# Which engine gives out the first small load: ScalarE in place of Sync

## The chip, the core and the metric

The kernel runs on one core of one Trainium2 chip. A core has TensorE (PE in the profile, with its weight loads as PEld), VectorE (DVE), ScalarE (ACT), GpSimd (POOL) and SyncE (SP). Each has its own queue of instructions, worked off in order, and they wait for each other through semaphores. Transfers between the chip's memory (HBM) and the on-chip buffers are given out by an engine's queue as DMA issues and carried out by 16 DMA engines. The metric is device time in microseconds for one execution. Before the change the median of three runs is 377.19 us (376.98 to 377.27).

## The reference

One decoding step: two sequences (B = 2), one token each, width D = 512. The token is normalised and goes through attention over a window of 2048 cached positions in 32 heads of 128, and through a bilinear feed-forward block of width F = 1376; both are added to the input. All numbers are 32-bit floats.

```python
W = min(4096, max(256, Sk // 4))                       # Sk = 8192, so W = 2048
xn = _layernorm(x, axis=-1)
q = (xn @ wq).reshape(B, 1, 32, 128).transpose(0, 2, 1, 3)
k = k_cache[:, :, Sk - W:, :]
v = v_cache[:, :, Sk - W:, :]
scores = jnp.einsum("bhqd,bhkd->bhqk", q, k) * (128 ** -0.5)
p = _softmax(scores, axis=-1)
o = jnp.einsum("bhqk,bhkd->bhqd", p, v)
attn = o.transpose(0, 2, 1, 3).reshape(B, 1, 4096) @ wo
h = jnp.einsum("bsd,df->bsf", xn, w_gate) * jnp.einsum("bsd,df->bsf", xn, w_up)
out = x + attn + jnp.einsum("bsf,fd->bsd", h, w_down)
```

Every cached key and value and every weight is used once, so some 160 MB go from HBM to the chip and little is computed on each byte.

## The kernel before

All inputs but the last rows of w_down are laid out as one long stream in HBM, in the order in which the kernel wants them. `blocks()` (line 86) lists the pieces: one small load, with the key `("f", 0)`, and then big loads of up to 128 x 15872 numbers (some 8 MB), with keys `("s", i)`. The small load goes to a tile of its own, `first`, 128 x 542 numbers: x, two small tables of ones (`pick`, `rows`) and the columns of wq for head 0. The big ones go to tiles called `step`, of which there are three buffers (`BUFS = 3`).

`pump()` (line 175) gives out loads as long as a buffer is free. It is called once at the start, where it gives out `first` and three big loads, and then from `done()` (line 198) each time that all fields of a big load have been used. All of these are issued by Sync, line 196. Behind the first call, line 213, Sync also issues four small loads of the last rows of w_down into `wd_tail`. Sync's queue is in order, so a load waits in it for its buffer, and the loads behind wait as well.

The first big load holds the rest of wq for heads 1 to 3 and the keys of heads 0, 1 and 2. The second holds the gate and up weights and the keys of head 3, the third values and more.

The work around the start runs like this. VectorE sums x from `first`, TensorE spreads the sums over the partitions with a matrix of 1/512 (`mean_w`), VectorE subtracts and squares, TensorE sums again, ScalarE takes the square root, VectorE scales, and copies the normalised token out to a wide tile `xnb`. Then `project_first(0)` (line 272) multiplies `xnb` with the wq of head 0 into `tr` on TensorE. From there, for each head, `products` (line 304) multiplies the keys with the query on VectorE, in place, `sums` (line 312) reduces them to scores on VectorE and then marks the keys as used; softmax follows on GpSimd and ScalarE, and the weighted sum of the values and the output projection on TensorE. When `sums(2)` is done the first buffer is free and Sync can issue the fourth big load into it.

Most instructions pass through a helper (`InOrder`, line 113) which keeps each engine's program in the order of the code, so the profile gives line 128 for nearly all of them; they are told apart by their tiles. The order of heads and of the big loads is worked out ahead by `groups()` and `packed()`; neither has to do with the small load.

Of the kernel before, what the change touches and what calls it, by code (L numbers as in the profile page):

```python
# [143 lines left out]
def kernel(  # L144
# [7 lines left out]
    pe, dve, act, sp = (InOrder(tc, e) for e in (nc.tensor, nc.vector, nc.scalar, nc.sync))  # L152
# [17 lines left out]
    tiles, used, left, got = {}, {}, {}, {}  # L170
# [4 lines left out]
    def pump():  # L175
        nonlocal held
        while todo:
            key, fields, at = todo[0]
            if key not in tiles:
                if key[0] == "f":  # L180
                    n = sum(w for _, _, w in fields)
                    tiles[key] = const.tile([P, n], F32, name="first")
                elif held == BUFS:
                    return
                else:
                    held += 1
                    tiles[key] = steps.tile([P, STEP], F32, name="step")
                used[key] = 0
            todo.pop(0)
            c0 = used[key]  # L190
            for kind, i, w in fields:
                got[kind, i] = (tiles[key][:, used[key] : used[key] + w], key)
                used[key] += w
            c1 = used[key]
            src = stream[at : at + P * (c1 - c0)].rearrange("(p i) -> p i", p=P)
            sp.dma_start(tiles[key][:, c0:c1], src)

    def done(kind, i):
        nonlocal held
        _, key = got.pop((kind, i))  # L200
        left[key] -= 1
        if left[key] == 0 and key[0] != "f":
            del tiles[key]
            held -= 1
            pump()

    pump()
    xT = got["x", 0][0].rearrange("p (b c) -> p b c", b=B)
    pick = got["pick", 0][0].rearrange("p (r s b) -> p r s b", s=2, b=B)
# [472 lines left out]
```

## Time and profile before

| | |
|---|---|
| median of three runs | 377.19 us (376.98 to 377.27) |
| profiled execution: span from first to last instruction | 375.6 us |
| the same execution's time beyond its span | not given; the median lies 1.6 us above the span |
| VectorE busy | 294.5 us, 78% |
| TensorE busy | 256.8 us, 68% |
| ScalarE busy | 57.1 us, 15% |
| moved by DMA | 159.70 MB, mean 425 GB/s over the span |
| Sync's DMA queue q1 | 159.54 MB, 98.5% of the 16 engines' span |
| small load `first` | 271.0 KB, issue to landing 2.8 us |

In the profile "DMA step<-in_stream_dram" is a big load and "DMA first<-in_stream_dram" the small one. SPq is Sync's queue giving out a DMA; the time beside it is that of the issue, and not of the transfer. In the DMA table q1 is the queue of the loads that Sync gives out, q8 and q14 are fetches of instructions; a row has packets, megabytes, and the time of the packets as a share of 16 engines over the stretch asked for. A packet counts with its whole time in the slice in which it begins, so over short stretches a share can be above 100%. The slices divide the stretch asked for into 40 equal parts.

### The profile page before, as it was taken

The numbers are of one execution on the slowest core, as the hardware profiler recorded it, in microseconds if no ns is written. First come the engines' busy times: TensorE is split into PE (matmuls) and PEld (weight loads), VectorE is DVE, ScalarE is ACT, GpSimd is POOL, SyncE is SP. The second block draws the span as 40 slices with busy tenths as digits, with TensorE's granted clock in tenths as the row PEclk, the third lists the DMA queues.
The fourth block names the chain that finished last, engine by engine and source line by source line (L and its number), as shares of the span: only waits on it lengthen the run. The fifth ranks groups of instructions, "written<-read, shape, count | busy, mean of one in ns | idle before, by whom it ended". The sixth has DMA issues, their size and how long they took to land.

```text
span 375.6 us, 2894 instructions
## 1 busy us (share of the span) xinstructions
PE 256.8 (68%) x1106; PEld 89.1 (24%) x1106; DVE 294.5 (78%) x144; ACT 57.1 (15%) x259; POOL 25.2 (7%) x74
## 2 busy tenths in 40 slices
PE   3166696884587881685858905896556864699896
PEld 3132123231222220121222202222211221133243
DVE  3069999369979569999369999894699999999750
ACT  1002011110201210021112002112010210112131
POOL 1000000000001000000100000010000000000010
PEclk9999697799576897598968875889666898689999
DMA  8999999999999999999999999999999999999995
GB/s 344 419 444 466 452 414 440 433 433 434 421 427 433 433 433 440 435 426 433 433 433 429 433 433 440 433 435 433 433 440 433 441 433 433 433 433 413 419 415 229
DMA packets 4092, 159.70 MB, mean 425 GB/s; under 512 B 462, under 2 KB 718, under 8 KB 1136
## 3 DMA queue, kind: packets, MB, share of 16 engines
q1 hardware_dynamic: 4080, 159.54, 98.5%
q8 instruction: 8, 0.13, 0.1%
q14 instruction: 4, 0.03, 0.0%
HBM read 159.47 MB, written 0.07 MB: 425 GB/s over the span
## 4 chain that ended last, share of the span: by engine, by line
DMA 65%; PE 18%; DVE 14%; ACT 1%; issue 1%; SPq 0%; DVEq 0%
DMA step<-in_stream_dram 65%; DVE s L128 7%; DVE step L128 7%; PE o_ps L128 6%; PE q L128 6%; PE acc L128 4%; PE tr L128 2%; ACT o_sb L128 1%; ACT oT L128 0%; DVE m L128 0%; SPq L128 0%; DVE o_out L128 0%; DVE rec L128 0%; DVEq L128 0%
## 5 line engine op out<-in xcount | busy, mean ns | idle before, releaser
L128 DVE TENSOR_TENSOR step<-step,q 128x4096 f32<-128x4096 f32 x31 | 136.8, 4412 | 45.1 <-DMA step<-in_stream_dram 41.1
L128 DVE TENSOR_REDUCE s<-step 128x32 f32<-128x4096 f32 x32 | 141.4, 4419 | 1.1
L128 PE MATMUL o_ps<-step,p 128*16 128x512 f32 x512 | 77.3, 667 | 47.6 <-DMA step<-in_stream_dram 47.5
L128 PE MATMUL q<-step,xnb 128*128 128x512 f32 (+1 forms) x128 | 74.2, 727 | 32.2 <-DMA step<-in_stream_dram 32.2
L128 PEld LDWEIGHTS q<-step,xnb 128*128 128x128 f32 x128 | 28.5, 238 | 81.4 <-issue 65.7
L128 PE MATMUL acc<-step,oT 128*2 128x512 f32 (+1 forms) x88 | 37.9, 590 | 8.6 <-ACT oT L128 8.6
L128 PE MATMUL tr<-first,o_sb 128*128 128x2 f32 (+4 forms) x190 | 29.5, 274 | 15.7 <-ACT o_sb L128 11.9
L128 PEld LDWEIGHTS o_ps<-step,p 128*16 128x16 f32 x512 | 13.6, 100 | 100.8 <-DMA step<-in_stream_dram 57.4
L128 PEld LDWEIGHTS tr<-first,o_sb 128*128 128x128 f32 (+2 forms) x190 | 26.9, 216 | 40.6 <-ACT o_sb L128 34.8
L128 ACT COPY o_sb<-o_ps 128x512 f32<-128x512 f32 x23 | 13.5, 585 | 147.4 <-PE o_ps L128 147.4
L322 POOL PARTITION_ALL_REDUCE mm<-m x32 | 11.4, 357 | 242.1 <-DVE rec L128 136.5
L128 ACT ACTIVATE nm<-mm 128x2 f32<-128x2 f32 x32 | 6.6, 206 | 127.4 <-POOL mm L322 127.4
L128 ACT ACTIVATE p<-s,nm 128x16 f32<-128x16 f32 x64 | 19.1, 300 | 1.0
L338 POOL PARTITION_ALL_REDUCE sum<-rs x32 | 12.7, 398 | 96.3 <-ACT p L128 96.3
L128 PE MATMUL o_ps<-step,xn 128*2 128x512 f32 (+1 forms) x48 | 14.8, 676 | 6.0 <-DMA step<-in_stream_dram 6.0
L128 DVE TENSOR_TENSOR step<-step,tr 128x4096 f32<-128x4096 f32 x1 | 4.4, 4422 | 15.4 <-DMA step<-in_stream_dram 15.4
L128 ACT ACTIVATE oT<-tr,rec 128x1 f32<-128x1 f32 x64 | 12.1, 260 | 27.7 <-PE tr L128 27.7
L128 ACT ACTIVATION_READ_ACCUMULATOR p<-s,nm 128x1 f32 x64 | 11.9, 187 | 0.0
L128 PE MATMUL q<-xnb,mean_w 128*128 128x512 f32 (+4 forms) x26 | 10.5, 512 | 0.0
L128 PEld LDWEIGHTS acc<-step,oT 128*2 128x2 f32 x88 | 4.4, 88 | 21.4 <-ACT oT L128 12.1
L128 DVE RECIPROCAL rec<-sum 128x2 f32<-128x2 f32 x32 | 5.0, 155 | 3.8 <-POOL sum L338 3.8
L128 PE MATMUL acc<-step,hT 128*2 128x128 f32 (+2 forms) x72 | 7.2, 308 | 0.0
(41 smaller groups left out, 43.6 us busy)
## 6 DMA issues: line engine op xcount, KB each, us to landing
step<-in_stream_dram SPq DMA_DIRECT2D x15, 7936.0 KB, 32.2
step<-in_stream_dram SPq DMA_DIRECT2D x1, 7808.0 KB, 39.1
step<-in_stream_dram SPq DMA_DIRECT2D x1, 7680.0 KB, 21.1
step<-in_stream_dram SPq DMA_DIRECT2D x1, 7552.0 KB, 57.8
step<-in_stream_dram SPq DMA_DIRECT2D x1, 4864.0 KB
step<-in_stream_dram SPq DMA_DIRECT2D x1, 3328.0 KB, 19.4
step<-in_stream_dram SPq DMA_DIRECT2D x1, 2304.0 KB, 24.5
step<-in_stream_dram SPq DMA_DIRECT2D x2, 1024.0 KB, 18.0
```

The source lines that it names most:

```text
L128: made = call(*args, **kwargs)
L322: nc.gpsimd.partition_all_reduce(mm, m, P, bass_isa.ReduceOp.max)
L338: nc.gpsimd.partition_all_reduce(sum_t[h], rs, P, bass_isa.ReduceOp.add)
```

## The change

The small load is issued by ScalarE; all other loads stay with Sync.

```diff
@@ -193,7 +193,7 @@
                 used[key] += w
             c1 = used[key]
             src = stream[at : at + P * (c1 - c0)].rearrange("(p i) -> p i", p=P)
-            sp.dma_start(tiles[key][:, c0:c1], src)
+            (act if key[0] == "f" else sp).dma_start(tiles[key][:, c0:c1], src)
```

`key[0] == "f"` is true for the small load alone. The layout of the stream, the tiles and all waits are as before. On Sync, at the head of its program, stood before (the first row is the jump into the kernel's body, `128x542` the small load, the wider ones big loads):

```order
L677 UNCONDITIONAL_BRANCH
L128 DMA first<-in_stream_dram 128x542
L128 DMA step<-in_stream_dram 128x15360
L128 DMA step<-in_stream_dram 128x15616
L128 DMA step<-in_stream_dram 128x15104
L128 DMA wd_tail<-in_tail_dram 25x512
L128 DMA wd_tail<-in_tail_dram 7x512
```

And in the same place now:

```order
L677 UNCONDITIONAL_BRANCH
L128 DMA step<-in_stream_dram 128x15360
L128 DMA step<-in_stream_dram 128x15616
L128 DMA step<-in_stream_dram 128x15104
L128 DMA wd_tail<-in_tail_dram 25x512
L128 DMA wd_tail<-in_tail_dram 7x512
```

The small load is gone and the rest of Sync's program follows one place earlier. On ScalarE, also at the head, stand now (the loads of tables of functions are its own; `st<-tr,eps_t` is the square root of the normalisation, `nm` and `p` belong to the softmax of head 0):

```order
L677 UNCONDITIONAL_BRANCH
L128 DMA first<-in_stream_dram 128x542
L128 ACT_TABLE_LOAD
L128 ACTIVATE st<-tr,eps_t 128x2
L128 ACTIVATE nm<-mm 128x2
L128 ACT_TABLE_LOAD
```

The second row is new: ScalarE gives out the small load ahead of its first table load. The rest of ScalarE's program, and the programs of TensorE, VectorE and GpSimd, are the same.

## The prediction

> **What bounds the kernel now.** I read the page's slices first, then the DMA table of the long middle, the chain of waits at the start, and last the DMA table of very short stretches, where single rows of a transfer can be seen. The first fence has the page's DMA slices and the queue rows for 70 to 350 us.
>
> ```profile
> DMA  8999999999999999999999999999999999999995
> ...
> q1 hardware_dynamic: 2195, 120.92, 99.7%
> q8 instruction: 6, 0.10, 0.1%
> q14 instruction: 4, 0.03, 0.0%
> ```
>
> The 16 DMA engines are full from the second slice to the last but one, and between 70 and 350 us Sync's queue (q1) alone fills 99.7% of them. So the end of the program is the end of one stream of bytes: whatever takes time from the stream moves the end by as much, and work that does not hold up the stream costs nothing. The change touches only the first few microseconds of that stream. Here is the timeline up to 11 us, shortened, and two rows of the page's DMA issues.
>
> ```profile
> 0.72 1.28 ACT L128 ACT_TABLE_LOAD   x1 [0.72 <-PEq L663]
> 0.72 0.38 SPq L128 DMA_DIRECT2D first<-in_stream_dram  x1
> 1.15 1.37 SPq L128 DMA_DIRECT2D step<-in_stream_dram  x3
> 3.54 0.16 DVE L128 TENSOR_REDUCE st<-first 128x2 f32<-128x8 f32 x1 [0.88 <-DMA first<-in_stream_dram]
> 5.62 0.26 ACT L128 ACTIVATE st<-tr,eps_t 128x2 f32<-128x2 f32 x1 [3.62 <-PE tr L128]
> 7.11 3.75 PE L128 MATMUL tr<-first,xnb 128*128 128x128 f32 x16 [1.53 <-issue]
> ...
> step<-in_stream_dram SPq DMA_DIRECT2D x1, 7680.0 KB, 21.1
> ...
> first<-in_stream_dram SPq DMA_DIRECT2D x1, 271.0 KB, 2.8
> ```
>
> The small load lands at 0.72 + 2.8 = 3.5 us. The normalisation and the query of head 0 follow and are done at 7.11 + 3.75 = 10.86 us, that is 7.35 us after the landing. The first big load lands only at 1.15 + 21.1 = 22.3 us. So before the change 11.4 us of slack lie between the query of head 0 and the keys that it meets. The chain of waits shows what VectorE does from there (its rows up to the first buffer's return), with Sync's timeline row of the load that takes the buffer and VectorE's waits between 70 and 79 us.
>
> ```profile
> 22.38 4.43 DVE step L128
> 26.84 4.43 DVE s L128
> ...
> 44.90 4.43 DVE s L128
> ...
> 49.39 0.36 SPq L128 DMA_DIRECT2D step<-in_stream_dram  x1
> ...
> DVE step L128 <- DMA step<-in_stream_dram: 7.8, 1, 7.8
> ```
>
> Three heads one behind the other, 22.38 to 49.33 us (44.90 + 4.43), 26.95 us, then Sync gives out the fourth big load into the freed buffer at 49.39 us. Later VectorE waits 7.8 us for that load, so a delay of VectorE up to that size is swallowed, provided the stream does not run dry meanwhile.
>
> **The start of the stream.** The DMA table for 0 to 4 us, in 40 slices of 0.1 us:
>
> ```profile
> GB/s 0 0 0 0 0 0 0 0 0 0 0 0 0 0 0 0 0 152 130 65 130 217 152 152 369 412 434 918 5067 701 1865 1229 0 614 0 0 0 0 0 0
> DMA packets 160, 1.26 MB, mean 315 GB/s; under 512 B 16, under 2 KB 16, under 8 KB 144
> ```
>
> A packet counts in the slice in which it begins. The 144 - 16 = 128 packets of 2168 bytes are the rows of the small load, eight for each DMA engine; the 16 under 512 bytes are the landing marks; the other 16 are the first rows (61440 bytes) of the first big load. The small rows begin in the slice from 1.7 us, 1.0 us after the issue at 0.72. The big rows begin between 2.7 and 3.4 us, although they were issued at 1.15 and could have begun at about 2.15: they wait behind the small rows, not for Sync. So Sync's 0.43 us (1.15 - 0.72) is not itself on the path. What can be won is that the small rows take 1.0 to 1.6 us, while 0.277 MB would take 0.64 us at the 433 GB/s of the middle (120.92 MB in 280 us is 432): 0.4 to 0.9 us if big rows fill the gaps, say 0.6.
>
> **What the change does, part by part.** (1) One issue leaves Sync's queue; three big and four tail issues move up by 0.43 us. Nobody waits for Sync's own time there, as shown. (2) ScalarE's queue gains one issue of 0.38 us ahead of its table load of 1.28 us, which then ends at 2.4 us instead of 2.0. Its first user starts at 5.62 us; 3.2 us of cover are left, and more if the small load is late. Price: zero. (3) Both queues now issue at 0.72 us, so the rows of both should reach the DMA engines at 1.7 us, and from there each engine has eight rows of 2 KB in one ring and rows of 60 KB in another.
>
> No row shows two such rings side by side. The nearest is the fetch of instructions, which breaks into the same stream from a queue of its own. The fence has the DMA queue rows of windows 0.10 us wide, where the share times 1.6 is the time of the packets that begin in it: first an undisturbed row (from 93.60), then a fetch (from 93.41, with the begin of another engine's row), then the stream's rows that follow fetches (from 93.72, 105.61 and 205.83; from 253.46 two rows, one disturbed and one not).
>
> ```profile
> q1 hardware_dynamic: 1, 0.06, 146.4%
> ...
> q14 instruction: 1, 0.01, 19.3%
> ...
> q1 hardware_dynamic: 1, 0.06, 167.6%
> ...
> q1 hardware_dynamic: 1, 0.06, 185.1%
> ...
> q1 hardware_dynamic: 1, 0.06, 159.9%
> ...
> q1 hardware_dynamic: 2, 0.13, 314.6%
> ```
>
> An undisturbed row takes 2.34 us. The fetch of 8 KB takes 0.31 us, its bytes' worth. The row behind a fetch takes 2.68, 2.96, 2.56 and 5.03 - 2.34 = 2.69 us: 0.34, 0.62, 0.22 and 0.35 us too long, 0.38 in the mean. So the engine does change queues between two rows, and the stream pays at its return.
>
> From this two things follow. First, the small load no longer lands early. If each engine takes one row from each ring in turn, the eighth small row and its landing mark come just about when the eighth big row has gone, so the small load lands with the first big load, at about 22 us instead of 3.5. The Trainium skill says so outright: "DMA: Bandwidth & Descriptors", section "Queues, rings and completion order", has each DMA engine go round robin over the queues that have work, a packet at a time. By that rule the small load lands near 22 us; the fetch rows above agree, though they show single packets only.
>
> Then VectorE begins its first head at 22.3 + 7.35 = 29.7 instead of 22.4 us, 7.3 us later, and the fourth big load is issued 7.3 us later, near 56.7, its rows ready 1.0 us after (as at the start), near 57.7 us. Does the stream have work until then? The DMA slices from 57.30 to 58.42 us, 0.028 us each, show where the engines go over to the fourth load (2268 and more is one of its 63488-byte rows):
>
> ```profile
> GB/s 0 73 0 0 4608 0 0 4682 0 2268 146 0 2341 146 146 0 146 2414 0 146 146 73 2414 146 73 4535 2414 73 0 2414 73 0 2341 73 0 2268 73 0 0 2268
> ```
>
> They go over between 57.4 and 58.4 us. So the first engines would wait 0.3 us, the last none: 0.1 in the mean, with the first rows' latency 0.2. That is the price of a VectorE delay of 7.3 us; each further microsecond of it would cost nearly a whole one. The 7.8 us that VectorE waited for the fourth load then cover the delay, so nothing is late behind it.
>
> Second, the returns. One or two small rows may slip through before the first big row, so I take seven returns per engine at 0.38 us, 2.7 us; all engines pay it and the engine's own rate leaves nothing to catch up with. The ends: nothing (two filled rings may overlap where a lone fetch cannot), and 8 x 0.62 = 5.0 us. I take the 8 KB fetches since they are nearest in size to 2 KB; the 16 KB fetches of q8 are farther.
>
> **The sum.** Start -0.6, returns +2.7, dry stream +0.2: +2.3 us. The profiled span of 375.6 us becomes 377.9. The median of the runs, 377.19, lies 1.6 us above that span; with the same 1.6 us the time is 379.5 us.
>
> **The rivals.** (a) The small load is late, but the change of rings is free. Then -0.6 + 0.2 = -0.4, between -0.9 and +0.2: 376.8 us, the other side. It decides if a return costs less than (0.6 - 0.2) / 7 = 0.06 us. For it: at the start both rings stand full, while a fetch comes alone. Against it: four of four rows behind a fetch were slower by 0.22 us or more. (b) The small load is not held up, because ScalarE's rows reach the engines a microsecond ahead or the engine empties a short ring first. VectorE keeps its times, and 0 to 0.6 us are won: 376.9 us. Against it: ScalarE's first instruction and Sync's first issue both stand at 0.72 us, so no head start is to be seen. A page would have this outcome too: the Trainium skill, "DMA: Bandwidth & Descriptors", section "Issuing engines are not separate DMA queues", says that issuing from several engines saves only the sequencer's time for the issue; here that would be at most 0.43 us, about 376.8 us. (c) The small load is held still longer, a big row of 2.3 us or more beyond the first big load, because its landing mark waits for one more turn. Each such row makes VectorE late beyond its cover: 379.5 + 2.2 = 381.7 us, or 379 with free returns.
>
> **Chances.** The forecast (late, with paid returns) 0.50; (a) 0.25; (b) 0.17; (c) 0.08. A difference of 0.2%, 0.75 us, is about what a measurement can tell from none. The forecast and (c) are slower; of (a) about a quarter is faster and a little slower, of (b) two fifths faster: faster 0.13, same 0.27, slower 0.60. The forecast's own range is 378.1 to 382.0: 377.2 - 0.6 with seven returns of 0.22 (1.5) and no dry stream, to 377.2 - 0.4 with eight of 0.62 (5.0) and 0.2. The range reaches below to (a) and (b) near their best, 376.5, and above past the forecast's end and (c) to 382.5.
>
> **What would show it.** Right: the small load's time to landing near 21 us instead of 2.8; the normalisation and the query of head 0 at 22 to 30 us; VectorE's first head near 30; the first big load landing 1 to 3 us later than 22.3; a short dip of the DMA near 58; VectorE's 7.8 us wait nearly gone; everything behind shifted by a constant. Wrong: the small load landing before 10 us; the first big load landing earlier than 22.3 us; or a dry stretch of several microseconds near 58, which would mean that VectorE's delay, not the returns, is the price.

## The result and the profile after

The changed kernel takes 379.17 us (median of four runs, 378.79 to 379.5) against 377.19 us before: 1.0052 times as long, with a 95% interval of 1.0040 to 1.0064. A few runs of the kernel before, in the sessions below, took 5 us or more longer than its others (382.54 us against a median of 377.08 in one session), which widens some intervals and hardly moves the medians. The profiled execution of the changed kernel spans 377.7 us against 375.6. In it the small load behaves as forecast. The fence has the queue rows of the page, two rows of the page's DMA issues, and the timeline's rows for the start.

```profile
q1 hardware_dynamic: 3936, 159.26, 97.9%
q10 hardware_dynamic: 144, 0.28, 0.2%
...
step<-in_stream_dram SPq DMA_DIRECT2D x1, 7680.0 KB, 21.5
...
first<-in_stream_dram ACTq DMA_DIRECT2D x1, 271.0 KB, 21.7
...
0.72 0.40 ACTq L128 DMA_DIRECT2D first<-in_stream_dram  x1
0.72 1.32 SPq L128 DMA_DIRECT2D step<-in_stream_dram  x3
22.47 0.16 DVE L128 TENSOR_REDUCE st<-first 128x2 f32<-128x8 f32 x1 [19.80 <-DMA first<-in_stream_dram]
26.04 3.75 PE L128 MATMUL tr<-first,xnb 128*128 128x128 f32 x16 [1.53 <-issue]
29.83 4.42 DVE L128 TENSOR_TENSOR step<-step,tr 128x4096 f32<-128x4096 f32 x1 [3.88 <-PE tr L128]
```

ScalarE's loads have a queue of their own, q10, and both first issues begin at 0.72 us. The small load lands at 0.72 + 21.7 = 22.4 us instead of 3.5, the first big load at 0.72 + 21.5 = 22.2 (22.3 before), and VectorE begins head 0 at 29.83 instead of 22.38 us, 7.45 us late.

How the two rings share an engine is seen between 9 and 11 us, in the DMA table's queue rows (packets that begin there, MB, their time as a share of 16 engines):

```profile
q1 hardware_dynamic: 16, 0.98, 113.5%
q10 hardware_dynamic: 16, 0.03, 4.5%
```

Each of 16 engines began one big row and one small one. A big row took 1.135 x 32 / 16 = 2.27 us, a small one 0.09. In the trace's records the two kinds alternate row by row from 4.5 to 21.9 us. Yet 110 of the 112 big rows that began after 4 us took the 2.27 us that rows of this length take undisturbed. The return to the stream costs nothing here. The Trainium skill ("DMA: Bandwidth & Descriptors", "Queues, rings and completion order") has each engine take turns between the queues a packet at a time, typically 9 to 17 descriptors; the trace agrees on the turns, and here one turn is one row.

The cost comes later, at the fourth big load. The fence has, of the changed kernel, Sync's issue of it, the DMA slices from 57.5 to 59.5 us (0.05 us each; 1270 and more is a row of the fourth load), and the stage from 57 to 61 us; the stage's row of before is the last one (busy time of PE, PEld, DVE, ACT and POOL, granted clock, DMA share, GB/s).

```profile
56.83 0.36 SPq L128 DMA_DIRECT2D step<-in_stream_dram  x1
...
GB/s 0 41 41 82 41 123 1393 41 1393 2622 2581 123 1352 1311 82 1352 0 82 1270 82 1311 0 1270 0 0 1270 0 0 0 0 0 0 0 0 0 0 0 1270 1270 0
...
57.00:61.00 4.00, 0.00 (x0) 0.00 (x0) 4.00 (x2) 1.36 (x6) 0.75 (x2) 0.82 1.03 382
```

```profile
57.00:61.00 4.00, 1.69 (x8) 1.10 (x6) 3.26 (x5) 0.38 (x3) 0.35 (x1) 0.89 1.22 509
```

The issue at 56.83 us is 7.44 us later than before. The first rows of the fourth load begin between 57.8 and 59.4 us, 1.0 to 2.6 us after it, in all engines but one, which is still at its last row of the third load until 59.56 us. Before they began between 57.4 and 58.4, also in all engines but one, without a pause. In the mean of the 16 engines the first rows begin 0.48 us later than before (58.44 instead of 57.96) and then take 2.91 instead of 2.48 us, so about half of the loss here is a late beginning and half is slower first rows. In the stage rows of 382 GB/s begin instead of 509; that is a rough sign, since a row counts where it begins. The other end of the chain is VectorE's timeline, here of the changed kernel (first fence) and of before: its wait for the last full load, and its last instruction.

```profile
342.94 4.42 DVE L128 TENSOR_TENSOR step<-step,q 128x4096 f32<-128x4096 f32 x1 [0.46 <-DMA step<-in_stream_dram]
375.00 0.29 DVE L128 COPY o_out<-acc 128x128 f32<-128x128 f32 x1 [8.57 <-PE acc L128]
```

```profile
340.81 4.42 DVE L128 TENSOR_TENSOR step<-step,q 128x4096 f32<-128x4096 f32 x1 [0.45 <-DMA step<-in_stream_dram]
372.85 0.29 DVE L128 COPY o_out<-acc 128x128 f32<-128x128 f32 x1 [8.57 <-PE acc L128]
```

From the landing to the end it is 32.0 us in both. The landing is 2.13 us late, and that is the whole loss.

The page's chain of waits of the changed kernel seems to say otherwise: it runs through TensorE from 324 us to the end, without a wait. But TensorE's weight load for the load that lands near 360 us still waits for the DMA, in the changed kernel (first) and before:

```profile
362.27 0.13 PEld L128 LDWEIGHTS o_ps<-step,p 128*16 128x16 f32 x8 [0.32 <-DMA step<-in_stream_dram]
```

```profile
360.13 0.13 PEld L128 LDWEIGHTS o_ps<-step,p 128*16 128x16 f32 x8 [0.53 <-DMA step<-in_stream_dram]
```

In both it begins 0.04 us after the last of that load's 16 landing marks (362.23 and 360.09 us). TensorE is close behind the load in this execution, in which its granted clock is 0.50 from 350 to 353 us. In the second profile of the changed kernel, further below, the clock stays at 1.00 there, TensorE waits for the loads again, and the end is still as late as the landing.

To see where the lateness arose I added up the stream from the trace's records of single rows, a row's bytes spread evenly over its time:

| the stream has moved | before | after | late by |
|---|---|---|---|
| 4 MB | 11.89 us | 11.98 us | 0.1 |
| 22 MB | 53.44 | 53.55 | 0.1 |
| 26 MB | 62.85 | 63.75 | 0.9 |
| 100 MB | 233.68 | 234.67 | 1.0 |
| 140 MB | 326.03 | 327.04 | 1.0 |

So 0.1 us is lost at the start, 0.9 in the mean of the engines near 58 us, and from there to the landing at 342.9 us another 1.1 us that the mean does not show.

### The profile page after: what moved, and what is told of

It is laid out like the page before. It is cut to its first block, busy times and chain, and to the rows that moved or that the text cites. A ratio compares the mean times of both kernels' runs of the same rounds, so it can differ in the third digit from the quotient of the medians.

```text
span 377.7 us, 2894 instructions
## 1 busy us (share of the span) xinstructions
PE 255.8 (68%) x1106; PEld 90.2 (24%) x1106; DVE 294.3 (78%) x144; ACT 57.1 (15%) x259; POOL 25.1 (7%) x74
## 4 chain that ended last, share of the span: by engine, by line
DMA 50%; PE 27%; DVE 18%; issue 2%; ACT 2%; POOL 0%; SPq 0%
DMA step<-in_stream_dram 44%; DVE step L128 9%; PE o_ps L128 8%; DVE s L128 8%; PE q L128 7%; PE acc L128 6%; DMA first<-in_stream_dram 6%; PE tr L128 5%; ACT o_sb L128 1%; ACT oT L128 1%; DVE m L128 0%; ACT p L128 0%; ACT hT L128 0%; DVE o_sb L128 0%; DVE rec L128 0%
## 5 line engine op out<-in xcount | busy, mean ns | idle before, releaser
L128 PE MATMUL q<-step,xnb 128*128 128x512 f32 (+1 forms) x128 | 76.3, 744 | 28.0 <-DMA step<-in_stream_dram 28.0
L128 PEld LDWEIGHTS q<-step,xnb 128*128 128x128 f32 x128 | 29.3, 245 | 77.7 <-issue 72.2
L128 PE MATMUL tr<-st,mean_w 128*128 128x2 f32 x4 | 1.2, 364 | 23.3 <-DVE st L128 23.3
L128 PE MATMUL o_ps<-step,xn 128*2 128x512 f32 (+1 forms) x48 | 11.9, 548 | 0.0
L128 PE MATMUL q<-xnb,mean_w 128*128 128x512 f32 (+4 forms) x26 | 11.4, 548 | 0.0
## 6 DMA issues: line engine op xcount, KB each, us to landing
step<-in_stream_dram SPq DMA_DIRECT2D x1, 7680.0 KB, 21.5
step<-in_stream_dram SPq DMA_DIRECT2D x1, 7552.0 KB, 58.4
```

The costliest lines, as they stand in the source:

```text
L128: made = call(*args, **kwargs)
```

## The experiments

Three theories stood against each other. "Late": the small load's late landing makes VectorE late, so that the fourth big load is issued when the stream is running out. "Shared rings": the engines lose time while they change between two queues. "ScalarE": an issue from ScalarE costs by itself.

**Four small loads ahead of the first big one.**

```diff
+    for r0, r1 in ((0, FIVES), (FIVES, FT - 2), (FT - 2, FT - 1), (FT - 1, FT)):
+        sp.dma_start(wd_tail[r0:r1, :], tail[r0:r1, :])
     pump()                      # the small load from ScalarE, as with the change
...
-    for r0, r1 in ((0, FIVES), (FIVES, FT - 2), (FT - 2, FT - 1), (FT - 1, FT)):
-        sp.dma_start(wd_tail[r0:r1, :], tail[r0:r1, :])
```

> ScalarE still gives out the small load, but Sync gives out the four small wd_tail loads ahead of the first big one, so that the big rows come some 1.4 us after the small ones. Theory 'late' (the price is that the small load lands at 22 us, VectorE starts 7.4 us late and the fourth big load then finds the stream dry): the small load lands before 5 us and the time is that of before, 377.2 us (376.9 to 377.6). Theory 'shared rings' (the DMA engines lose time while two queues are worked in turn): little is shared either, so also near 377.2. Theory 'ScalarE' (an issue from ScalarE's queue itself costs): 379.2 as with the change.

Measured: 379.27 us (378.89 to 380.11), ratio 1.0059 (1.0044 to 1.0075). That is the number which theory "ScalarE" named, but not for its reason, as the timeline and one row of the chain of waits show:

```profile
2.04 1.30 SPq L128 DMA_DIRECT2D step<-in_stream_dram  x3
4.10 0.16 DVE L128 TENSOR_REDUCE st<-first 128x2 f32<-128x8 f32 x1 [1.44 <-DMA first<-in_stream_dram]
...
2.04 23.22 DMA step<-in_stream_dram
```

The small load landed early (VectorE used it at 4.10 us), but the first big load landed at 25.3 instead of 22.3 us. The whole stream was 1.55 us late at 22 MB, because Sync came to the first big load only at 2.04 us. I had put a new cost into the kernel by moving the four issues ahead, so this run tells none of the theories apart. It does show that a late first big load is not made up for: at 100 MB the stream is still 1.4 us late.

**The small load behind the first big one, all on Sync.**

```diff
-    out = [(("f", 0), first)] + [(("s", i), fields) for i, fields in enumerate(loads)]
+    out = [(("s", i), fields) for i, fields in enumerate(loads)]
+    out.insert(1, (("f", 0), first))
...
-        kind: np.zeros((P, w), a.dtype) for kind, _, w in blocks()[0][1][:3]
+        kind: np.zeros((P, w), a.dtype) for kind, _, w in blocks()[1][1][:3]
```

> Everything on Sync's one queue, but the small load behind the first big load, so that it lands at about 22.4 us without a second queue. 'Late': as with the change, 379.2 us (378.7 to 379.7), with a dry stretch near 58 us. 'Shared rings' and 'ScalarE': no second queue, so 377.2 us.

Measured: 380.09 us (378.63 to 380.91), ratio 1.0070 (1.0045 to 1.0094). One queue, no ScalarE, and about as slow as the changed kernel, with runs on both sides of its runs: VectorE began head 0 at 30.09 us, and in the stage from 57 to 61 us rows of 271 GB/s began. A late small load is enough.

**The changed kernel with a shorter way to the query.**

```diff
-    dve.tensor_reduce(st[:, 0, :], xT, axis=AX.X, op=ALU.add)
...
-    dve.reciprocal(st[:, 3, :], st[:, 2, :])
     xn = const.tile([P, NC, B], F32, name="xn")
-    dve.tensor_tensor(xn, xc.rearrange("p b c -> p c b"), ..., op=ALU.mult)
+    dve.tensor_copy(xn, xT.rearrange("p b c -> p c b"))
```

> The changed kernel with the normalisation left out (x itself goes to the projections; two matmuls, six VectorE instructions, the square root and with it one table load are gone). The way from the small load's landing to the query of head 0 is some 2.6 us shorter, so VectorE is late by about 4.8 instead of 7.4 us. 'Late': the fourth big load comes in time, 377.2 to 377.6 us. 'Shared rings' and 'ScalarE': the stream is disturbed as with the change, 379.2 us.

Measured: 377.32 us, ratio 1.0005 (0.9993 to 1.0018). The rows are VectorE's first use of the small load and the start of head 0, then the queue row of ScalarE's loads and the stage from 57 to 61 us:

```profile
22.68 0.17 DVE L128 COPY xn<-first 128x8 f32<-128x8 f32 x1 [20.02 <-DMA first<-in_stream_dram]
27.45 4.42 DVE L128 TENSOR_TENSOR step<-step,tr 128x4096 f32<-128x4096 f32 x1 [3.86 <-PE tr L128]
...
q10 hardware_dynamic: 144, 0.28, 0.2%
...
57.00:61.00 4.00, 0.00 (x0) 0.00 (x0) 3.97 (x2) 0.00 (x0) 0.00 (x0) 0.73 1.23 509
```

ScalarE issues, two rings are shared and the small load lands as late as with the change; only VectorE is 5.07 us late instead of 7.45. The stage is back at 509 GB/s, the stream is 0.1 us late at 22 MB as with the change and no later at 100 MB, and the loss is gone, to within what can be told. "Shared rings" and "ScalarE" fall.

**The kernel before with a late VectorE.** The copy to `xnb` is repeated, so the queries of head 0 come late, with the small load first on Sync as before. Three doses:

```diff
-    dve.tensor_copy(xnb, ...)
+    for _ in range(29):         # 27 and 35 in the two other runs
+        dve.tensor_copy(xnb, ...)
```

> The kernel before, its small load first on Sync, but the copy to xnb done 28 more times on VectorE (0.67 to 0.69 us each), so that head 0 starts near 29.8 us as with the change, and the stream is not touched. 'Late': 379.2 us (378.7 to 379.9). 'Shared rings' and 'ScalarE': 377.2 us.

> The kernel before with 26 extra copies to xnb, at 0.73 us each by the trace of the run with 28, so that head 0 starts at 29.8 us, the same moment as with the change (29.83), with the small load first on Sync and one queue. 'Late': the stream loses 0.8 us near 58 us as with the change, and the time is between 378.1 (only the mean loss) and 379.5 us (when the engine that is last is hit as well). If sharing two rings costs something beyond the lateness: 377.5 to 378.0 us, clearly under the changed kernel.

> 34 extra copies: head 0 starts at 35.7 us, 13.3 us late. 'Late' with a slope of one microsecond of stream for each microsecond beyond about 29.0 us: the stream loses 6.6 us and the time is 383.8 us (383.3 to 385). If the loss has a ceiling (one refilling of the DMA engines, whatever the delay): about as the run with 28 copies, 379.9 us.

Measured: with 28 more copies 379.9 us, ratio 1.0073 (1.0058 to 1.0088), where head 0 starts at 31.28 us and not at 29.8, since the copies took 0.73 us each; with 26, where head 0 starts at 29.87 us, 378.71 us (378.39 to 380.77), ratio 1.0045 (1.0017 to 1.0073); with 34 384.5 us, ratio 1.0179 (1.0127 to 1.0231). The stage from 57 to 61 us with 26, 28 and 34 copies more:

```profile
57.00:61.00 4.00, 0.00 (x0) 0.00 (x0) 4.00 (x3) 1.36 (x6) 0.75 (x2) 0.76 0.99 351
```

```profile
57.00:61.00 4.00, 0.00 (x0) 0.00 (x0) 3.97 (x4) 1.36 (x6) 0.75 (x2) 0.66 0.82 271
```

```profile
57.00:61.00 4.00, 3.49 (x12) 0.85 (x10) 3.97 (x2) 0.00 (x0) 0.00 (x0) 1.00 0.05 17
```

The same lateness without a second queue gives a loss that can't be told from the change's: 378.71 us with a range that holds all runs of the changed kernel. The loss grows with the dose and without a ceiling. Between 22 and 100 MB the stream loses 1.0, 2.4 and 6.8 us for head 0 at 29.87, 31.28 and 35.77 us: 5.8 us more for 5.9 us later, a slope of one, which leads back to a start near 28.9 us, 6.5 us late. By this line the stream has a cover of 6.5 us.

**A second copy of the small load.** It was meant to give the price of sharing by itself, with VectorE in time:

```diff
-    const.tile([P, PADS[0]], F32, name="pad0")
+    pad0 = const.tile([P, PADS[0]], F32, name="pad0")
...
             sp.dma_start(tiles[key][:, c0:c1], src)
+            if key[0] == "f":
+                act.dma_start(pad0[:, 0:c1], src)
```

> The kernel before, its small load first on Sync, and a second copy of the small load given out by ScalarE at the same time into an unused tile. VectorE is in time, and the second copy shares the engines with the first big load, row by row. The bytes are 0.28 MB more, 0.64 us. 'Late' (sharing free): 377.8 us (377.6 to 378.2). 'Shared rings' at 0.38 us for each return to the stream: 380 us or more.

Measured: 377.65 us (377.56 to 377.77), ratio 1.0005 (0.9978 to 1.0032); against the median of 377.08 in the same session it is 0.57 us for bytes worth 0.64. But the second copy did not share the engines with the first big load, as I had expected. In the trace's records its rows begin between 2.0 and 4.0 us and take turns with the small rows of `first`, and each engine begins its first big row only behind them, between 3.5 and 4.1 us. So the run shows that two short loads side by side cost no more than their bytes, and says nothing on turns with rows of 60 KB. What those cost is shown by the changed kernel (2.27 us for a big row behind a small one) and by the run with the shorter way, which takes the same turns and loses nothing.

**More stream ahead of the fourth load.** On top of the change, and then alone:

```diff
-    loads += [v(0) + wd(0) + [("wr", 0, HD)] + k(LAG + 1) + v(1)]
+    loads += [v(0) + wd(0) + [("wr", 0, HD)] + k(LAG + 1) + v(1) + [("wq", 5, CP)]]
...
-    loads += packed([f for _, fields, h in order for f in fields(h)])
+    loads += packed([f for _, fields, h in order for f in fields(h) if f[:2] != ("wq", 5)])
```

> The changed kernel with the wq columns of head 5 (128 x 512 numbers) moved from the fourth big load to the end of the third; the bytes are the same, but 0.6 us more of the stream stands ahead of the fourth load. 'Late': the dry stretch shrinks from 0.8 to 0.2 us in the mean, and the time to 377.4 to 378.6 us. Any theory in which the stream's start or the issue from ScalarE costs: 379.2 us as with the change.

> The kernel before with only the move of head 5's wq columns from the fourth to the third big load, the small load first on Sync as before. If the run with this move on top of the change was slow because the repacked loads make a slower end (TensorE's chain behind 337 us at half its clock): clearly above 377.2, 378 to 379 us. If the move is harmless by itself: 377.0 to 377.4 us, and that run's time came from the late small load after all.

Measured: with the change 379.55 us (377.91 to 380.4 over twelve runs), ratio 1.0050 (1.0023 to 1.0077), which is not the gain that I expected; alone 377.5 us, ratio 1.0019 (1.0003 to 1.0034), 0.45 us above the median of before in that session and slightly above the 377.0 to 377.4 us for a harmless move. The stream did lose less between 22 and 100 MB, 0.4 instead of 0.9 us. But the end no longer hangs on the stream alone. The stage from 349 to 355 us, with the move and the change (first) and with the move alone, and then TensorE's first matmuls on the load that lands near 360 us, with the move and the change:

```profile
349.00:355.00 6.00, 6.00 (x26) 2.03 (x30) 3.21 (x4) 0.72 (x4) 0.35 (x1) 0.72 0.96 414
```

```profile
349.00:355.00 6.00, 4.75 (x24) 0.89 (x23) 3.63 (x4) 0.57 (x1) 0.36 (x1) 1.00 0.97 417
```

```profile
362.24 1.91 PE L128 MATMUL o_ps<-step,p 128*16 128x512 f32 x16
```

TensorE is busy throughout at a granted clock of 0.72, where with the move alone it is at 1.00 and waits between its tasks. That alone does not set the run apart, since the first profile of the changed kernel has 6.00 us and 0.72 in this stage too. But here the load has landed at 361.15 us, and TensorE comes to it 1.09 us later, where in the changed kernel it is there 0.04 us after the landing. So about half of this run's loss is TensorE's. In this run the chain of waits goes through TensorE, with short steps on ScalarE, from 337 us to the end. Why the clock falls there, and how much of the twelve runs' spread it makes, stays open.

**The changed kernel twice more.**

> The changed kernel once more, for a second profile. If the end hangs on the landing of the last full load, that is on the last of the 16 DMA engines: VectorE's wait for that load near 342 us ends 32.0 us before the copy to o_out, as in the runs so far, and the landing is late by the stream's mean loss of 1.0 us plus a part of 0 to 2 us that changes from run to run. If the part beyond the mean loss is something fixed: the landing stands at 342.9 us again, 2.1 us after that of before.

> The changed kernel a third time, with the same expectation: 32.0 us from the landing of the last full load to the copy to o_out; landing near 342.9 us if the part beyond the mean loss is fixed, anywhere between 341.8 and 344 us if it changes from run to run.

Measured: 379.13 and 378.7 us. VectorE's wait for the last full load ended at 342.58 and 342.08 us, and `o_out` began 32.05 and 32.08 us later. In the first of the two TensorE idles 1.25 us before the load that lands at 354.04 us, so there the end hangs on the loads alone. The table sets the runs with the same big loads side by side. The stream's lateness is that at 100 MB, and the landing's is that of the last full load, both against before.

| kernel | head 0 starts | stream late | landing late | difference | landing to `o_out` |
|---|---|---|---|---|---|
| change | 29.83 | 1.0 | 2.13 | 1.15 | 32.06 |
| change, again | 29.59 | 0.8 | 1.77 | 1.0 | 32.05 |
| change, a third time | 29.54 | 0.9 | 1.27 | 0.4 | 32.08 |
| small load behind | 30.09 | 1.1 | 3.22 | 2.1 | 32.00 |
| four loads ahead | 25.36 | 1.4 | 2.78 | 1.4 | 32.03 |
| shorter way | 27.45 | 0.1 | 0.13 | 0.0 | 32.06 |
| 26 copies | 29.87 | 0.9 | 1.01 | 0.1 | 32.99 |
| 28 copies | 31.28 | 2.3 | 2.37 | 0.0 | 32.05 |
| 34 copies | 35.77 | 6.7 | 6.69 | 0.0 | 32.19 |
| second copy | 22.64 | -0.3 | 0.16 | 0.45 | 32.02 |

With 26 copies TensorE waited another 0.88 us for data near 370 us, behind the last full load; hence the 32.99. The difference is not fixed: 0.4 to 1.15 us in the changed kernel alone. A load has landed when the last of the 16 engines has its rows: in each of these runs TensorE's matmuls on the load near 360 us begin 0.04 or 0.05 us after the sixteenth landing mark. In the trace's landing marks of the load that lands near 360 us the sixteenth comes 0.50 us behind the eighth before, and 1.97 us after the change. The dry stretch does not hit the engines alike (their rows of the fourth load begin 1.0 to 2.6 us after the issue), and an engine that fetches instructions falls back too. Followed from row to row, the one that is last after the change restarted at 59.36 us, as one of the last, and fetched at 102.5 us. That such pairs make the difference is argued from these rows; no run was made that could choose the engine of a fetch, so it is not shown.

## Why the prediction was right in sum, and where not

The chain from the small load's landing to the fourth big load was right, and so was the sum (379.5 against 379.17 us). That the sum came out, and even its direction, is luck. The returns of 2.7 us do not exist, and without them the prediction's own terms give -0.4 us, a faster kernel. In their place stand two terms that it sized wrongly: the start, which won nothing (0.7 us), and the dry stretch with what follows from it (1.8 us).

- "The small load lands with the first big load, at about 22 us": right, 22.4 us. "VectorE begins its first head at 22.3 + 7.35 = 29.7": right, 29.83. "The fourth big load is issued 7.3 us later, near 56.7": right, 56.83. "The 7.8 us that VectorE waited for the fourth load then cover the delay": right, the wait between 70 and 79 us is gone.
- "Seven returns per engine at 0.38 us, 2.7 us": wrong, nothing. Big rows behind small ones take 2.27 us, and with the shorter way the same turns cost no time. The fetch of instructions was the nearest row, but a fetch comes as a lone packet; two filled rings are another case. Why a row behind a fetch takes longer and one behind a small row does not stays open. The condition that the prediction set for rival (a), a return under 0.06 us, is met.
- "0.4 to 0.9 us if big rows fill the gaps, say 0.6": wrong, 0.1 us is lost. The first big rows now begin at 1.7 us, but take 2.3 to 3.5 us instead of 2.27, where before they took up to 3.2; at 4 MB the stream is 0.1 us later than before.
- "0.1 in the mean, with the first rows' latency 0.2": the term that was too small, 0.9 us in the mean and up to 1.15 more by the time of the last full landing. The step that failed is "its rows ready 1.0 us after (as at the start)": 1.0 us holds for the first engine only, the last of those that stood idle began 2.6 us after the issue, their first rows also took 0.43 us longer in the mean, and the loads wait for the last engine. By the doses the cover ends at 6.5 us of lateness, and not at 7.3.
- Of the rivals, (a) had the mechanism (late, free returns) and the wrong price for the dry stretch, 376.8 us. (b) did not happen. (c) did not: the small load landed with the first big one and no row later.
- Of its signs, "the first big load landing 1 to 3 us later than 22.3" did not come: it landed at 22.2 us, and a landing before 22.3 stood among the signs of being wrong. That was the sign that the returns are free. "Everything behind shifted by a constant" did not come either: the stream is 1.0 us late in the mean and the last full load 2.13.

The round robin that the Trainium skill gives was borne out, with one row for a turn. That a turn is one row the prediction had assumed, and no row of its own showed it. The saving of the issue's time, by which the Trainium skill ("DMA: Bandwidth & Descriptors", "Issuing engines are not separate DMA queues") would have 376.8 us, was not measured: the change costs 2.0 us, because the short load loses its place ahead of the long one.

## What to carry to other kernels

A short load on which the first computation waits belongs in the same queue ahead of a long one: from a second queue its rows took turns here with rows of 60 KB, eight of either on each engine, and it landed when the long load did. Before such a load may come late, work out when the engine behind it next frees a buffer, and compare that with the moment at which the last of the DMA engines, not the first, can have new rows. Here 6.5 us of lateness cost nothing and every microsecond beyond cost one.

## What was not expected of the hardware

Two filled load rings on one DMA engine are shared without loss (2.27 us for a 61440-byte row in turn with 2168-byte rows), while a row behind an 8 KB fetch of instructions is 0.22 to 0.62 us too long. After an idle moment the engines do not begin a load together: 1.0 to 2.6 us after its issue in the changed kernel, and 1.0 to 1.8 us with 34 copies, where all 16 stood idle. And a delay that hits some engines more than others stays for the rest of the stream: in the changed kernel the sixteenth landing mark comes 2.17, 2.00 and 1.97 us behind the eighth at the loads that land near 343, 354 and 362 us, and the mean stream was 1.0 us late where the landing was up to 2.1 us late.
